# Attention followed by a mixture of experts: the handover reordered, places read sooner, a quarter of GpSimd's descriptor space, two buffers of results, and rows of small blocks in portions

## The chip, the cores and the metric

The kernel runs on one core of a Trainium2 chip. The metric is the device time of one execution in microseconds (us), as the median of several. Before the change three runs took 877.47, 880.67 and 881.1 us. One more execution was profiled; the rows quoted here come from it. Engines go by these names: PE is TensorE (PEld its weight loads), DVE is VectorE, ACT is ScalarE, POOL is GpSimd, SP is the engine that only issues transfers. A `q` behind an engine's name means its instruction queue.

## The reference

Inputs are q, k and v of 8 batches, 12 heads, 448 tokens and 64 columns in float32, a cap of 30, a router of 768 x 8 and, for 8 experts, w1 of 768 x 1024 and w2 of 1024 x 768.

```
scores = scale * q @ k^T;  scores = cap * tanh(scores / cap)
attn = exp(scores - max) / (sum + 1e-9);  y = attn @ v
x = y as 3584 tokens x 768
logits = x @ w_gate;  e = argmax(logits);  gate = softmax(logits)[e]
out[token] = gate * (relu(x @ w1[e]) @ w2[e])
```

Every token goes to one expert, so how many tokens an expert gets is known only after the router has seen them.

## The kernel before, in words

**Attention.** There are 8 batches of 6 pairs of heads, 48 pairs, each one step `n` of a loop. In a step TensorE makes the scores of a pair (L253, L260), ScalarE takes tanh and exp (L264, L273; one exponential of 128x1792 a pair for the first two thirds, one of 128x896 for the rest), VectorE and GpSimd add the probabilities for the row sums (`adds`, L282 on VectorE, L290 on GpSimd), TensorE multiplies with v into PSUM (`pv`, L309, L320), and VectorE copies the result out of PSUM (L336) and transposes it (`turn`, L347). The engines run an order that is written out by hand: each engine takes its instructions in the order in which the program issues them. Other work is hung into this loop with `at(step, when, function, ...)`; `do(step, when)` issues it. Within a step the order of the places is 0, scores, products with v of the pair before, 5, `adds` of the first half, second scores, loads, 3, second products with v, 6, `adds` of the second half, 1, 2.

**Routing.** Once a batch's six pairs are done (its step `n` is then the first of the next batch) it is normalised, routed and stored: `rec_v`, `rec_p`, `rec_c` (reciprocal sums), `log_v`, `log_p` (logits), `route_v` (argmax, L466 to L480), `place_p` (TensorE counts tokens before each one, L517 and L519), `place_v` (VectorE: each token's place in its expert's list, L529 to L538, which also moves `base`, the counts so far), `scale` (L505), `store` (rows to the DRAM array `xd`, on SP's queue) and `place_d` (GpSimd scatters the tokens' numbers into the DRAM lists `ids`, four indirect transfers a batch, L544). `log_p`, `place_p` and the router's products L372 share one PSUM bank, `ps_l`.

**Blocks.** The experts' work is cut into blocks of 448 tokens (large) or 256 (small) of one expert each. Two early blocks, -1 and -2, are chosen before attention is over (`first_block`, spread over steps by `decide`): -1 from the first 4 batches, so that its rows and weights are there when attention ends; -2 from the first 6. All later blocks come from a table made at the end; here their order is 0 to 4 (large), then two small ones. For a block, `load_ids` reads its part of the lists (an indirect transfer into `idt`, waiting for the scatters issued before it), `make_idx` turns it into row numbers (VectorE, L874), `load_x` gathers its rows into `xg` (14 indirect transfers for a large block, 8 for a small one, L802), `trans_x`, `high_x` and `low_x` transpose them and split them into a high and a low part (L910, L913, L917), and `load_w0` (SP, early blocks) or `load_w` (GpSimd, four indirect transfers) fetches weights, which `high` and `low` split (L843, L848). `up` is the first product with its relu (18 matmuls, L940; L945, L946), `down` the second (L970, L978), each in eight chunks. `evac` brings the result from PSUM into the tile `ys` (L1003, L1013), and `put` scatters it to the output (L812).

**The handover.** After step 47 the program goes on with block -1 by hand: `up(-1, 0)` while the last batch is still being routed, with the splits of the weights, the gathers of block -2 (`load_x(-2, ...)`) and the last batches' `place_d` between them.

**The expert loop.** While block j computes, GpSimd gathers the next block's rows and stores the results of the one before. In large blocks `moves` spreads both over the chunks: `XS` and `PS` say how many groups of rows go out at which chunk, and `step`, a one-column copy on GpSimd that reads a chunk's activation, holds GpSimd back until that chunk is there (L952).

Of the kernel before, what the change touches and what calls it, by code (L numbers as in the profile page):

```python
# [4 lines left out]
F32 = mybir.dt.float32  # L5
# [121 lines left out]
def attention_moe(tc, qT, kT, vL, capd, wgL, w1a, w1b, w2a, w2b, cst, cmk, out):  # L127
# [768 lines left out]
    def load_x(j, gs=None):  # L896
        xi = idt[j][0]
        rows = 4 * S * (B_FIRST[-1 - j] if j < 0 else B)
        for g in gs or range(groups(j)):
            gather(xg[:, g, :], xd[0:rows, :], xi[:, g : g + 1], rows - 1)  # L900
# [87 lines left out]
    def evac(j, cs=range(2)):  # L988
        y = m["y"]
        if cs[0] == 0:  # L990

            ys[j] = (
                ys0
                if j == -1
                else xg.rearrange("p q x -> p (q x)")
                if j == ORDER[-2]
                else m["yo"].tile([128, QB * XW], F32, name="ys")
            )
        o = ys[j]
        if large(j):  # L1000
            ov = o.rearrange("p (q k i) -> p q k i", k=KC, i=32)
            for k in range(KC):
                V.transpose(out=ov[:, :, k, :], in_=y[k][:, 0:LARGE].rearrange("p (q j) -> p q j", j=32))  # L1003
        else:
            ov = o[:, 0 : 2 * DM].rearrange("p (c a k i) -> p c k a i", c=2, a=4, i=32)
            for c in cs:
                for half in range(2):
                    src = y[2 * c + half][:, 0:384].rearrange("p (k a i) -> p k a i", a=4, i=32)
                    dst = ov[:, c, 3 * half : 3 * half + 3]
                    if half == 0:  # L1010
                        A.copy(out=dst, in_=src)
                    else:
                        V.tensor_copy(out=dst, in_=src)  # L1013
# [19 lines left out]
    def at(step, when, f, *a):  # L1033
        tasks.setdefault((step, when), []).append((f, a))
# [5 lines left out]
    for b in range(B):  # L1040

        n = b * NP + NP
        for g in range(1, NP, 2):
            i = b * NP + g
            at(i + 2, 5, sums, i)
        at(n, 5, logits, b, range(4))
        at(n + 1, 3 if b == B - 1 else 5, logits, b, range(4, NP))
        if b == B - 1:
            break
        at(n + 1, 6, rec_v, b)  # L1050
        at(n + 2, 3, rec_p, b)
        at(n + 2, 6, rec_c, b)
        at(n + 3, 0, log_v, b)
        at(n + 3, 6, log_p, b)
        at(n + 3, 1, route_v, b)
        at(n + 4, 5, route_s, b)
        at(n + 4, 3, place_p, b)
        at(n + 4, 6, route_g, b)
        at(n + 4, 1, scale, b, 0, V)
        at(n + 5, 0, scale, b, 1, V)  # L1060
        at(n + 5, 2, store, b, range(0, 2))
        at(n + 5, 1, place_v, b)
        at(n + 6, 2, store, b, range(2, 4))
        if b < B - 2:
            for q in range(4):
                at(n + (7 if b < 4 else 11 if b == 4 else 7), 1, place_d, b, q)
    at(1, 1, constants)
    at(n_first, 1, lambda: [None for _ in first_block(0)])
    at(n_first, 2, first_row, 0)
    for i in range(2 * FC):  # L1070
        at(n_first + 1 + i, 2, load_w0, -1, i)
    at(n_first + 2, 2, load_ids, -1)
    at(n_first + 3, 1, make_idx, -1)

    g = 0
    for i, w in enumerate((5, 5, 4)):
# [1 line left out]
        g += w  # L1078


    for n, k, last in ((8, 0, 1), (7, 1, 1), (6, 2, 1), (6, 3, 1), (4, 4, 2), (4, 5, 2)):
        at(n_pairs - n, 2, trans_x, -1, k)
        at(n_pairs - n + 1, 5, high_x, -1, k)
        at(n_pairs - n + last, 1 if last == 1 else 3, low_x, -1, k, V)
    at(n_pairs - 2, 2, split_w1, 0, G)

    second = first_block(1)

# [1 line left out]
        for _ in range(k):  # L1090
            next(second, 0)

    for n, k in ((6, 6), (4, 8), (1, 4)):
        at(n_pairs - n, 6, decide, k)
    at(n_pairs, 0, split_w1, 1, G)
    at(n_pairs, 6, decide, 100)
    for q in range(4):
        at(n_pairs, 1, place_d, B - 2, q)
    at(n_pairs, 1, load_ids, -2)

    for i in "hl":
        m["x" + i] = xp.tile([128, KC, LARGE], F32R, name="x" + i)
# [62 lines left out]
    do(n_pairs + 1, 3)  # L1165
    assert not tasks
    split(1, 2)
    make_idx(-2)
    load_x(-2, range(3))
    up(-1, 1)  # L1170
    rec_p(b)
    rec_c(b)
    log_v(b)
    split(1, 3)
    up(-1, 2)
    step(-1, 2)
    load_x(-2, range(3, 5))
    split(1, 4)
    log_p(b)
    route_v(b)  # L1180
    route_s(b)
    up(-1, 3)
    step(-1, 3)
    load_x(-2, range(5, 8))
    place_p(b)
    split(1, 5)
    place_v(b)
    up(-1, 4)
    step(-1, 4)
    load_x(-2, range(8, 10))  # L1190
    split(2, 0)
    turn(n_pairs - 2)
    turn(n_pairs - 1)
# [2 lines left out]
    w2s[3] = chunk(hw2, "w23")  # L1196
    up(-1, 5)
    step(-1, 5)
    load_x(-2, range(10, 12))
    split(2, 1)  # L1200
    route_g(b)
    scale(b, 0, V)
# [13 lines left out]
    wb = m["yo"] = pools("wb", **tw)  # L1216
    w2s[4] = chunk(wb, "w24")
    w25h = wb.tile([128, DM], F32R, name="w25h")
    ys0 = wb.tile([128, QB * XW], F32, name="ys")
    w26l = wb.tile([128, DM], F32R, name="w26l")  # L1220
    w2s[5] = [w25h, wb.tile([128, DM], F32R, name="w25l")]
    w2s[6] = [wb.tile([128, DM], F32R, name="w26h"), w26l]
# [4 lines left out]
    fill(4)  # L1227
    up(-1, 6)
    step(-1, 6)
    load_x(-2, range(12, 14))  # L1230
    for q in range(4):
        place_d(b, q)
    split(2, 5)
# [59 lines left out]

    XS, PS = (3, 3, 3, 3, 2, 0, 0), (0, 1, 1, 2, 2, 4, 4)

    def moves(j, n0, n1, f):
        if f > 0:
            step(j, f + 1)
        for load, n, what in ((True, n1, XS), (False, n0, PS)):
            g = sum(what[:f])  # L1300
            gs = range(g, min(g + what[f], groups(n) if load else QB))
            if load and gs:
                load_x(n, gs)
            elif gs:
                put(n, gs=gs)

    for i, j in enumerate(blocks):
        if i == 0:
            continue
        n0 = blocks[i - 1]  # L1310
        n1 = blocks[i + 1] if i + 1 < len(blocks) else None
        n2 = blocks[i + 2] if i + 2 < len(blocks) else None
        up(j, 0)
        if i == 1:
            splits(*late[0][:1])
        up(j, 1)
        splits_after(i, 0)
        if n1 is not None:
            make_idx(n1)
            load_w(n1, 1 if i > 1 else 0)  # L1320
            if not large(j):
                load_x(n1)
        if n2 is not None and not large(j):
            load_ids(n2)
        for f in range(FC):
            if large(j) and f < len(XS):
                moves(j, n0, n1, f)
            if 0 < f:
                splits_after(i, f)
                if f == 2 and i == 1:  # L1330
                    load_w(n1, 1)
            if n1 is not None:
                splits_in(i, f)

            down(j, f, range(2) if n1 is not None or f < 3 else range(1))
            if f + 2 < FC:
                if f + 2 == FC - 1 and n1 is not None:
                    for k in range(XT):
                        trans_x(n1, k)
                up(j, f + 2)  # L1340
            if f + 2 == FC and n1 is not None:
                split_xs(n1)
            if f == 4:
                if n2 is not None:
                    if large(j):
                        load_ids(n2)
                if not large(j):
                    put(n0)
            if f == (6 if i == 1 else 4) and n2 is not None:
                load_w(n2, 0)  # L1350
        if n1 is not None:
            evac(j)
# [93 lines left out]
```

## Time and profile before

| | |
|---|---|
| runs | 877.47, 880.67, 881.1 us |
| profiled execution | 879.77 us, span 877.8 us |
| TensorE | 830.4 us busy, 4492 matmuls |
| VectorE | 556.9 us busy |
| ScalarE | 483.4 us busy |
| GpSimd | 460.5 us busy |
| mean granted TensorE clock | 0.984 |
| moved | 117.96 MB |

The span runs from the first to the last instruction; the rest of an execution's time lies around it. Attention takes the first 370 us or so, the experts the rest. The chain of work that ended last is TensorE for 53% of the span. In rows of the timeline the first two numbers are the start and the duration, and brackets hold the idle time of the engine just before the instruction and what ended it. In rows of waits stand the waiting engine and line, what it waited for, the total, the number of times and the longest.

### The profile page before, as it was taken

How to read it: one execution, taken by the hardware profiler on the slowest of the kernel's cores; microseconds unless marked ns; L12 is line 12 of the kernel's file. 1: busy time of each engine (PE TensorE's matmuls, PEld its weight loads, DVE VectorE, ACT ScalarE, POOL GpSimd, SP SyncE). 2: the span in 40 equal slices, each digit the busy share in tenths (PEclk: the TensorE clock that was granted, in tenths of full speed). 3: DMA queues.
4: the chain of work that ended last, by engine and by line, in shares of the span. 5: the costliest groups of instructions: out<-in, count | busy, mean ns of one | idle time of the engine just before them, and what ended most of it. 6: DMA issues, size and time to landing. Idle time of an engine off the chain costs nothing.

```text
span 877.8 us, 12128 instructions
## 1 busy us (share of the span) xinstructions
PE 830.4 (95%) x4492; PEld 555.2 (63%) x4492; DVE 556.9 (63%) x912; ACT 483.4 (55%) x573; POOL 460.5 (52%) x380
## 2 busy tenths in 40 slices
PE   8999999999969999689999999999999999999993
PEld 3233332323222322169999989899999999999993
DVE  3559797979966899958682844734635536437620
ACT  7999998989876989413342532423323324233420
POOL 1423353434347654534348767578577675665710
PEclk9999999999999999899999999999999999999997
DMA  6131545555556655336645272454431124544210
GB/s 211 69 127 66 186 80 172 98 154 101 187 100 200 223 162 136 80 93 163 134 167 206 77 300 61 176 193 165 169 100 55 33 63 175 186 180 166 81 43 34
DMA packets 46883, 117.96 MB, mean 134 GB/s; under 512 B 8241, under 2 KB 27091, under 8 KB 43744
## 3 DMA queue, kind: packets, MB, share of 16 engines
q1 hardware_dynamic: 30688, 57.01, 23.5%
q0 software_dynamic: 15840, 59.86, 19.3%
q8 instruction: 37, 0.61, 0.3%
q14 instruction: 30, 0.25, 0.1%
q10 hardware_dynamic: 288, 0.23, 0.1%
HBM read 101.40 MB, written 22.36 MB: 141 GB/s over the span
## 4 chain that ended last, share of the span: by engine, by line
PE 53%; DVE 8%; issue 4%; POOL 2%; DMA 2%; ACT 1%; POOLq 0%; DVEq 0%; ACTq 0%
PE ph L940 23%; PE y L970 17%; PE y L978 4%; DVE p L282 2%; PE po L320 2%; PE sp L253 2%; DVE ys L1003 1%; PE po L970 1%; PE z L970 1%; DMA idt<-ids,ti 1%; POOL out L812 1%; DMA ids<-tok,slots 1%; DVE xl L917 1%; PE ps_l L970 1%; PE ps_s L970 1%
## 5 line engine op out<-in xcount | busy, mean ns | idle before, releaser
L290 POOL TENSOR_TENSOR p<-p,pr 64x896 f32<-64x896 f32 x47 | 107.3, 2282 | 189.8 <-DVE p L282 114.7
L945 ACT ACTIVATE hb<-ph 128x448 fp32r<-128x448 f32 (+1 forms) x69 | 35.1, 508 | 285.9 <-PE ph L940 197.4
L946 DVE SCALAR_TENSOR_TENSOR hb<-ph,hb 128x448 fp32r<-128x448 f32 (+1 forms) x69 | 39.4, 574 | 191.2 <-ACT hb L945 191.2
L264 ACT ACTIVATE pt<-sp,qsc 128x896 f32<-128x896 f32 x144 | 139.2, 1001 | 33.6 <-PE sp L253 33.0
L802 POOL DMA_INDIRECT xg<-xd,xi x114 | 136.5, 1198 | 37.8 <-issue 31.7
L253 PE MATMUL sp<-qr,kr 64*128 64x448 f32 x576 | 134.9, 572 | 3.0 <-ACT pr L264 1.5
L273 ACT ACTIVATE pt<-pt,capt 128x1792 f32<-128x1792 f32 x94 | 132.9, 1413 | 2.3
L320 PE MATMUL po<-pt,vr 128*64 128x448 f32 x576 | 130.9, 562 | 0.0
L812 POOL DMA_INDIRECT out<-ys,xi x98 | 107.7, 1099 | 29.2 <-issue 27.4
L253 PEld LDWEIGHTS sp<-qr,kr 64*128 64x128 f32 x576 | 47.1, 185 | 85.3 <-issue 46.7
L282 DVE TENSOR_TENSOR p<-pt 128x896 f32<-128x896 f32 x48 | 71.3, 1485 | 31.1 <-ACT pt L273 25.5
L320 PEld LDWEIGHTS po<-pt,vr 128*64 128x64 f32 x576 | 33.2, 137 | 79.3 <-issue 78.8
L282 DVE TENSOR_TENSOR p<-p,pt 128x896 f32<-128x896 f32 x48 | 54.5, 1135 | 20.7 <-ACT pt L273 19.8
L544 POOL DMA_INDIRECT ids<-tok,slots x32 | 36.4, 1136 | 12.6 <-issue 5.8
L913 ACT CAST xh<-xt 128x448 fp32r<-128x448 f32 (+1 forms) x54 | 27.0, 531 | 20.8 <-DVE xt L910 20.7
L336 DVE COPY ot<-po 128x448 f32<-128x448 f32 x48 | 29.5, 615 | 10.4 <-PE po L320 10.2
L309 PE MATMUL po<-pr,vr 64*64 64x448 f32 x192 | 27.3, 570 | 7.1 <-DVE ot L336 7.1
L802 POOL DMA_INDIRECT w1r<-in_w1b,widx x7 | 10.0, 1435 | 44.8 <-DVE w17l L848 44.5
L910 DVE STREAM_TRANSPOSE xt<-xg 128x448 f32<-128x448 f32 (+1 forms) x54 | 30.2, 584 | 0.8
L917 DVE TENSOR_TENSOR xl<-xt,xh 128x448 fp32r<-128x448 f32 (+1 forms) x54 | 28.8, 559 | 0.0
L1003 DVE STREAM_TRANSPOSE ys<-y 128x448 f32<-128x448 f32 x36 | 19.8, 613 | 13.2 <-DMA out<-ys,xi 7.7
L952 POOL COPY pace<-hb 128x1 f32<-128x1 f32 x40 | 13.7, 342 | 27.0 <-ACT hb L945 26.9
(420 smaller groups left out, 1946.1 us busy)
## 6 DMA issues: line engine op xcount, KB each, us to landing
vr<-in_vL SPq DMA_DIRECT2D x24, 448.0 KB, 6.1
kr<-in_kT SPq DMA_DIRECT2D x23, 448.0 KB, 3.4
qr<-in_qT SPq DMA_DIRECT2D x23, 448.0 KB, 4.6
xd<-yt SPq DMA_DIRECT2D x20, 336.0 KB, 6.5
xd<-w2r SPq DMA_DIRECT2D x12, 336.0 KB, 6.8
w1r<-in_w1a SPq DMA_DIRECT2D x8, 384.0 KB, 5.3
w1r<-in_w1b SPq DMA_DIRECT2D x8, 384.0 KB, 5.7
w2r<-in_w2a SPq DMA_DIRECT2D x8, 384.0 KB, 5.6
```

The source lines that it names most:

```text
L253: PE.matmul(sp[:, j, 0:S], kr[r, i, c], qr[r, i, :], start=True, stop=True)
L264: A.activation(out=x, in_=sp[:, 0:2, 0:S], func=AF.Tanh, scale=qsc)
L273: A.activation(out=pt[:, lo:hi, :], in_=pt[:, lo:hi, :], func=AF.Exp, scale=capt)
L282: V.tensor_tensor(out=p4, in0=pt[:, 0:2] if half == 0 else p4, in1=pt[:, 2 * half + 2 : 2 * half + 4], op=ALU.add)
L290: e.tensor_tensor(out=p4[r], in0=p4[r], in1=rests[n // 2][r], op=ALU.add)
L320: PE.matmul(po[64 * j : 64 * j + 64, 0:S], vr[:, n % 2 * 6 + 3 * j + t, :], pt[:, 2 * t + j], start=n == t == 0, stop=t == 2 and n > 0,)
L802: G.indirect_dma_start(out=dst, out_offset=None, in_=src, in_offset=bass.IndirectOffsetOnAxis(ap=idx.bitcast(U32), axis=0), bounds_check=b ...
L812: i = G.indirect_dma_start(out=dst, out_offset=bass.IndirectOffsetOnAxis(ap=idx.bitcast(U32), axis=0), in_=src, in_offset=None, bounds_che ...
L917: e.tensor_tensor(out=m["xl"][:, k, 0:n], in0=xts.pop((j, k)), in1=m["xh"][:, k, 0:n], op=ALU.subtract)
L940: PE.matmul(ph, w[:, c], x[:, k, 0:n], start=i == 0, stop=i == 3 * KC - 1)
L946: V.scalar_tensor_tensor(out=hl, in0=ph, scalar=0.0, in1=hh, op0=ALU.max, op1=ALU.subtract)
L970: PE.matmul(y[k][:, 0:LARGE], w[:, c], h, start=f == 0 and i == 0, stop=f == FC - 1 and i == 2)
```

## The change

Five things change at once.

- *Places read sooner.* `place_p` and `place_v` of every batch but the last change their order against the adds of their step (one later by most of a step, one a little sooner). The scatters of batch 3 go out two steps sooner, those of the other early batches at place 2 of the same step, and the list of block -1 is read one step sooner. In `decide`, and in the transposes and splits of block -1's rows, the steps are shared out anew.
- *Handover reordered.* The first two weight splits of w1 have their low part made by VectorE and not by GpSimd. The scatters of batch 6 are no longer issued before the list of block -2 is read, but after the gathers of its rows. `make_idx(-2)` and the first gathers stand after `log_v` of the last batch, and all fourteen gathers are out one chunk sooner.
- *A quarter of GpSimd's descriptor space.* `dynamic_dma_scratch_size` is 4096 bytes a partition; without the argument it is 16384.
- *Two buffers of results.* The tile `ys` gets two buffers of 10,752 bytes a partition.
- *Rows of small blocks in portions.* `moves` is used in small blocks too, with `XN` and `PN`: the next block's rows by two, the results of the large block before by 4, 5 and 5; a small block's results go out at chunk 4.

```diff
-                else m["yo"].tile([128, QB * XW], F32, name="ys")
+                else m["yo"].tile([128, QB * XW], F32, name="ys", bufs=2)
...
-        at(n + 4, 3, place_p, b)
+        at(n + 5, 5, place_p, b)
...
-        at(n + 5, 1, place_v, b)
+        at(n + 5, 6, place_v, b)
         at(n + 6, 2, store, b, range(2, 4))
         if b < B - 2:
             for q in range(4):
-                at(n + (7 if b < 4 else 11 if b == 4 else 7), 1, place_d, b, q)
+
+                at(n + (5 if b == B_FIRST[0] - 1 else 11 if b == 4 else 7), 2, place_d, b, q)
...
-    at(n_first + 2, 2, load_ids, -1)
-    at(n_first + 3, 1, make_idx, -1)
+    at(n_first + 1, 2, load_ids, -1)
+    at(n_first + 2, 1, make_idx, -1)
...
-    for n, k, last in ((8, 0, 1), (7, 1, 1), (6, 2, 1), (6, 3, 1), (4, 4, 2), (4, 5, 2)):
+    for n, k, late in ((8, 0, 0), (7, 1, 0), (6, 2, 0), (6, 3, 0), (6, 4, 1), (5, 5, 0)):
         at(n_pairs - n, 2, trans_x, -1, k)
-        at(n_pairs - n + 1, 5, high_x, -1, k)
-        at(n_pairs - n + last, 1 if last == 1 else 3, low_x, -1, k, V)
-    at(n_pairs - 2, 2, split_w1, 0, G)
+        at(n_pairs - n + 1 + late, 5, high_x, -1, k)
+        at(n_pairs - n + 1 + late, 1, low_x, -1, k, V)
+    at(n_pairs - 2, 2, high, 1, 0)
+    at(n_pairs - 1, 1, low, 1, 0)
...
-    for n, k in ((6, 6), (4, 8), (1, 4)):
+    for n, k in ((6, 3), (4, 10), (2, 6)):
         at(n_pairs - n, 6, decide, k)
-    at(n_pairs, 0, split_w1, 1, G)
+    at(n_pairs, 0, high, 1, 1)
     at(n_pairs, 6, decide, 100)
-    for q in range(4):
-        at(n_pairs, 1, place_d, B - 2, q)
     at(n_pairs, 1, load_ids, -2)
+    at(n_pairs, 1, low, 1, 1)
...
     split(1, 2)
-    make_idx(-2)
-    load_x(-2, range(3))
     up(-1, 1)
     rec_p(b)
     rec_c(b)
     log_v(b)
+    make_idx(-2)
+    load_x(-2, range(3))
...
-    load_x(-2, range(10, 12))
+    load_x(-2, range(12, 14))
+    for q in range(4):
+        place_d(b - 1, q)
...
-    load_x(-2, range(12, 14))
     for q in range(4):
         place_d(b, q)
...
+    XN, PN = (2, 2, 2, 2, 0, 0, 0), (0, 0, 0, 0, 4, 5, 5)
+
     def moves(j, n0, n1, f):
         if f > 0:
             step(j, f + 1)
-        for load, n, what in ((True, n1, XS), (False, n0, PS)):
+        xs, ps = (XS, PS) if large(j) else (XN, PN)
+        for load, n, what in ((True, n1, xs), (False, n0, ps)):
+            if n is None:
+                continue
+            if not load and not large(n):
+                if f == 4:
+                    put(n)
+                continue
...
-            if not large(j):
-                load_x(n1)
...
-            if large(j) and f < len(XS):
+            if f < len(XS):
                 moves(j, n0, n1, f)
...
-                if not large(j):
-                    put(n0)
...
-    nc = bacc.Bacc("TRN2", target_bir_lowering=False, num_devices=1)
+    nc = bacc.Bacc("TRN2", target_bir_lowering=False, num_devices=1, dynamic_dma_scratch_size=4096)
```

More of the change, by code (lines that the diff above doesn't have):

```diff
@@ L1176, in attention_moe @@
     step(-1, 2)
-    load_x(-2, range(3, 5))
+    load_x(-2, range(3, 6))
     split(1, 4)
@@ L1183, in attention_moe @@
     step(-1, 3)
-    load_x(-2, range(5, 8))
+    load_x(-2, range(6, 9))
     place_p(b)
@@ L1189, in attention_moe @@
     step(-1, 4)
-    load_x(-2, range(8, 10))
+    load_x(-2, range(9, 12))
     split(2, 0)
@@ L1218, in attention_moe @@
     w25h = wb.tile([128, DM], F32R, name="w25h")
-    ys0 = wb.tile([128, QB * XW], F32, name="ys")
+    ys0 = wb.tile([128, QB * XW], F32, name="ys", bufs=2)
     w26l = wb.tile([128, DM], F32R, name="w26l")
```

## The prediction

> **What bounds the kernel now.** I read the busy time by stretch first, then GpSimd, VectorE and TensorE in order of time where TensorE is not full, then the list of waits. Columns of the first view: stretch, length, busy time (and instructions) of TensorE, weight load, VectorE, ScalarE and GpSimd, then granted clock, DMA share, GB/s.
>
> ```profile
> 0.00:240.00 240.00, 232.70 (x1338) 73.19 (x1340) 183.47 (x283) 215.97 (x206) 87.88 (x49) 1.00 0.46 133
> 240.00:300.00 60.00, 52.43 (x289) 15.74 (x287) 41.58 (x68) 45.24 (x43) 38.52 (x26) 0.94 0.57 157
> 300.00:360.00 60.00, 53.43 (x316) 16.48 (x312) 56.03 (x101) 54.10 (x56) 27.20 (x17) 1.00 0.49 144
> 360.00:400.00 40.00, 30.96 (x162) 21.48 (x155) 26.32 (x53) 8.92 (x14) 21.00 (x17) 0.87 0.44 106
> 400.00:860.00 460.00, 456.75 (x2380) 424.52 (x2380) 249.00 (x409) 158.70 (x256) 283.94 (x271) 1.00 0.40 137
> ```
>
> Attention up to 240 us keeps TensorE 97% and ScalarE 90% busy; the experts from 400 to 860 us keep TensorE 99% busy. There, an edit can win only the 3.25 us that are missing. The loose time lies between: 7.6 us idle in 240 to 300, 6.6 in 300 to 360, 9.0 in 360 to 400, and two of these stretches also run at a granted clock below 1. The parts below are ordered by the place they touch.
>
> **The change part by part.** Sums go against the profiled execution: span 877.8 us, 879.77 with what lies around it, 0.9 below the 880.67 median of the three runs shown.
>
> *A. Places read sooner, first early block.* Time, duration, engine, line; in brackets idle time before it and its releaser.
>
> ```profile
> 219.53 1.07 DVE L282 TENSOR_TENSOR p<-p,pt 128x896 f32<-128x896 f32 x1
> 237.64 2.09 POOL L290 TENSOR_TENSOR p<-p,pr 64x896 f32<-64x896 f32 x1 [7.53 <-DVE p L282]
> 241.38 1.07 DVE L282 TENSOR_TENSOR p<-p,pt 128x896 f32<-128x896 f32 x1
> 243.60 0.97 POOL L544 DMA_INDIRECT ids<-tok,slots  x1 [0.30 <-DVE lt L427]
> 244.88 0.92 POOL L544 DMA_INDIRECT ids<-tok,slots  x1 [0.30 <-issue]
> 249.98 1.79 ACT L273 ACTIVATE pt<-pt,capt 128x1792 f32<-128x1792 f32 x1
> 253.50 1.05 POOL L802 DMA_INDIRECT idt<-ids,ti  x1 [4.93 <-DMA ids<-tok,slots]
> 257.43 1.79 ACT L273 ACTIVATE pt<-pt,capt 128x1792 f32<-128x1792 f32 x1
> 259.30 0.23 DVE L874 TENSOR_SCALAR xi<-idt,kc 128x14 int32<-128x14 int32 x1 [7.64 <-DMA idt<-ids,ti]
> 263.11 1.76 PE L309 MATMUL po<-pr,vr 64*64 64x448 f32 x4 [7.12 <-DVE ot L336]
> 269.43 1.01 ACT L264 ACTIVATE pt<-sp,qsc 128x896 f32<-128x896 f32 x1 [10.21 <-PE sp L253]
> 273.34 1.79 ACT L273 ACTIVATE pt<-pt,capt 128x1792 f32<-128x1792 f32 x1
> DMA to landing us min/median/max: 6.8/8.9/13.8
> ```
>
> The last `place_d` of batch 3 is issued at 244.88 and lands by 253.5; only then may GpSimd read the list (`load_ids`), which lands at 259.3. VectorE stands 7.64 us in `make_idx`, with the PSUM copies of attention queued behind it, so TensorE stands 7.12 and then ScalarE 10.21. From one long exponential (L273, one a pair of heads) to the next this pair takes 273.34 - 257.43 = 15.91 us, the pair before it 257.43 - 249.98 = 7.45, so the stall is worth 8.5, and 10.2 if ScalarE's wait counts whole.
>
> Afterwards `place_v` of batch 3 stands before the add at 219.53, which moves that add to about 220.5, and its four `place_d` go out behind GpSimd's add of 2.1 us, from about 224 on, 1.28 apart (244.88 - 243.60), the last one at 228. They land (median 8.9) at 237, at worst at 242. `load_ids` follows GpSimd's add that ends at 239.7, and takes 5.8 (253.5 to 259.3) as here: 245.5, or 248 behind late scatters. VectorE asks for it after its add that ends at 242.45. A wait of 3 us remains, 5.5 at worst; ScalarE runs a pair ahead of VectorE here (its exponential of 249.98 is used by the add after 259.30), which hides part of such a wait. Putting the stall's whole worth at 10.2 and what still shows at 1.7, I take 8.5; the bounds are 3.0 (8.5 - 5.5) and 10.2. The five GpSimd issues move ahead of two of its adds, which start some 5 us later; TensorE reads those adds a pair (7 us) later.
>
> After A's stall the 240 to 300 row shows a clock of 0.94. The Trainium skill, "TensorE: Matmul & The Clock Gate" (Part 1: The HAM clock gate), puts the drop to half rate after an idle window of about 3.4 us; by it the remaining wait of 3 costs no clock. The trace agrees with the long stalls (7.12 us idle, then 0.06 x 60 = 3.6 us of clock lost); if the remainder still set it off, A would be 3.6 less, by the row, 4.9.
>
> *F. `place_p` and `place_v` swapped around, all batches.*
>
> ```profile
> PE ps_l L372 <- DVE base L531: 8.9, 5, 5.8
> PE ps_l L517 <- DVE ob L480: 4.4, 3, 2.4
> ```
>
> Waits in total, times, longest. The router matmul L372 reuses the bank that `place_v` reads; `place_v` now precedes an add instead of following it. The place matmul L517 moves most of a pair later and stops waiting for its one-hots. Without the two longest (C, B) that is 3.1 + 2.0 = 5.1 of TensorE time. ScalarE at 90% is close behind, so I take 2.0 (0 to 5.1).
>
> *B. Steps 42 to 47.* The 2.4 wait above (it falls at 351) disappears; two row transposes, their splits and four small decisions move ahead by one or two pairs. VectorE is 56.03 of 60 us busy in 300 to 360, so it gives little back: 1.5 (0 to 2.4).
>
> *C. End of attention: the first two weight splits leave GpSimd.*
>
> ```profile
> 362.19 3.12 POOL L848 TENSOR_TENSOR w10l<-w1r,w10h 128x768 fp32r<-128x768 f32 x1
> 363.57 4.46 DVE L282 TENSOR_TENSOR p<-pt 128x896 f32<-128x896 f32 x1
> 369.61 1.72 PE L372 MATMUL ps_l<-ot,wg 128*32 128x448 f32 x8 [5.81 <-DVE base L531]
> 372.87 0.47 PE L940 MATMUL ph<-xh,w10h 128*128 128x448 f32 x1
> 380.07 0.95 DVE L848 TENSOR_TENSOR w12l<-w1r,w12h 128x768 fp32r<-128x768 f32 x1
> ```
>
> VectorE's add takes 4.46 against 1.07 for its like (241.38) while GpSimd makes w10l and then w11l; behind it `place_v` is late, and TensorE stands 5.81. Both splits now cost VectorE 0.95 each (w12l), behind `place_v`; TensorE needs them for its first two expert products, the second one 3.7 us after the first. The add returns 3.4, `place_v` loses the decisions ahead of it: L372 starts near 365.7, 3.9 sooner, and L372 with the last products runs at full clock (3.26 from 369.61 to 372.87; about 2 undisturbed). 5.2 in all; at least 2 if the add stays slow for another reason, at most 5.81 + 1.3 = 7.1.
>
> *D. Second early block: places of batch 6 no longer before its list; `make_idx` behind `log_v`.*
>
> ```profile
> 382.40 1.05 POOL L802 DMA_INDIRECT idt<-ids,ti  x1 [6.68 <-DMA ids<-tok,slots]
> 385.78 0.23 DVE L874 TENSOR_SCALAR xi<-idt,kc 128x14 int32<-128x14 int32 x1 [4.76 <-DMA idt<-ids,ti]
> 389.51 0.49 PE L446 MATMUL ps_l<-lr,cs 128*128 128x112 f32 x2 [3.23 <-DVE lr L441]
> 395.34 7.55 PE ph L940 x36
> 417.52 3.72 PE ph L940 x18
> ```
>
> The list waits 6.68 for four scatters it does not need, VectorE 4.76 for the list, TensorE 3.23 for `log_v`. From 372.87 four first products end at 395.34: 22.5 us. At 3.7 each (417.52) they need 14.9, and the products between them (12 of the width of L372, of which 8 took 1.72 at a reduced clock, and some small ones) at most 2.6: 17.5; I leave 0.4 for the split that now follows `make_idx`: 4.6 (1.7 to 5.0). The list has 10 us until VectorE asks, against 3.4 (382.40 to 385.78). The four scatters stand later on GpSimd, after all 14 row gathers; nothing of this block reads them, and the next list still waits for those of batch 7 behind them. SP's loads for this block wait, as before, for the splits that free their slots. The row gathers queue behind `make_idx`, now some 6 us sooner than at 385.78.
>
> *E. Two result buffers.*
>
> ```profile
> PE y L970 <- DVE hb L946: 1.9, 2, 1.1
> PE y L978 <- DVE hb L946: 1.2, 1, 1.2
> 502.76 3.29 DVE L1003 STREAM_TRANSPOSE ys<-y 128x448 f32<-128x448 f32 x6
> 562.59 3.31 DVE L1003 STREAM_TRANSPOSE ys<-y 128x448 f32<-128x448 f32 x6 [3.70 <-DMA out<-ys,xi]
> 621.28 3.30 DVE L1003 STREAM_TRANSPOSE ys<-y 128x448 f32<-128x448 f32 x6 [2.56 <-issue]
> 796.29 3.30 DVE L1003 STREAM_TRANSPOSE ys<-y 128x448 f32<-128x448 f32 x6 [2.92 <-PE ph L940]
> ```
>
> Block results wait for the stores of the block before them; behind this wait stands the copy that the next products need, and TensorE loses 0.8 + 1.1 + 1.2 = 3.1. The 0.8 (502.76) had no wait ahead of it, only splits, and stays: 2.3 (0 to 3.1).
>
> *Portions for small blocks.* The gathers and stores of the two small blocks are spaced by `step`; they stay under the small blocks' products, and the end is set by the last products and their stores, which keep their order: 0. Without that cover the last stores come later by a portion of five, 5 x 1.28 = 6.4 us.
>
> *A quarter of the descriptor space.*
>
> ```profile
> DMA to landing us min/median/max: 2.1/3.5/10.3
> w2r<-in_w2b,widx POOLq DMA_INDIRECT x7, 9.8
> w1r<-in_w1b,widx POOLq DMA_INDIRECT x7, 7.6
> POOL w1r L802 <- DVE w17l L848: 44.5, 6, 8.6
> ```
>
> GpSimd issues 1.28 us apart (A) and gathers land within 10.3, so 8 are under way at most. No row shows an issue that waits for space: the old space held 8 or more, a quarter of it 2 or more. Taken at 0, as nothing queues on the whole; the price when it doesn't is the second rival. The Trainium skill, "DMA: Bandwidth & Descriptors" (The descriptor swizzle), counts 9 read and 9 write descriptors per engine for a 128-partition transfer, of 16 bytes; 4,096 bytes would then hold, as an estimate, 14 to 28 transfers, and the cost stays 0.
>
> Sum: 8.5 + 2.0 + 1.5 + 5.2 + 4.6 + 2.3 = 24.1; 879.77 - 24.1 = 855.7. All lower bounds: 6.7, giving 873.1; all upper ones: 32.9, giving 846.9.
>
> **The rivals.** *Half the stalls move on.* The scatters of A land at the slow end (13.8) and VectorE, full in 300 to 360, stays the bound up to 370: A 3.0, B 0, C 2, the others whole: 13.9, 865.9. For it speaks VectorE's 56 of 60; against it that its longest instruction there loses its cause.
>
> *Descriptor space runs short: slower.* If a pair of weight gathers plus rows fill the quarter, GpSimd stands until they land. A block of 58.7 us (562.59 to 621.28) holds 33 issues (14 gathers, 14 stores, one list, four weights) of 1.28 = 42, so 16.5 are free, 7.4 of them (44.5 / 6) in one wait before w1b. Both weight pairs awaited cost 2 x (7.6 + 9.8 - 2.6) = 29.6, 13.1 over, in six blocks 79: 935. It decides once such waits add up to over 16.5 a block. Against it: 8 under way, and gathers whose rows are single long pieces.
>
> *ScalarE sets attention's pace, and the handover only shifts idle time to the experts:* A and F give 3, C and D are lost again to late weights (loads and splits of the second block don't start sooner): within 0.5%, about 877. Against it: TensorE is full from 400 on without waiting for weights.
>
> **How the numbers follow.** Forecast 855.7 with its own range 848 to 862: 0.64. Half the stalls: 0.2. Descriptor space: 0.07. Nothing gained: 0.06. The remaining 0.03 is a faster end below 848. The range 848 to 867 takes in the first two. Half a per cent, about what a measurement tells from no change, is 4.4 us: faster 0.87, same 0.06, slower 0.07.
>
> **What would show it.** A: no wait over 3 us before `xi` near 242, clock 1.00 in 240 to 300. C: the add before `place_v` near 1.1 us, no GpSimd row of L848. D: no TensorE wait for `lr`. E: no wait of L1003 for stores. Space: waits before GpSimd issues beyond 0.3. It is wrong if the span between the last exponential and the first full expert product doesn't shrink by some 10 us.

## The result and the profile after

The changed kernel takes **852.12 us** (median of four runs, 850.72 to 854.53) beside 879.07 for the kernel before on the same chip (875.05 to 881.1): ratio 0.9705, 95% interval 0.9671 to 0.9739. The profiled execution took 851.22 us with a span of 849.2, 28.7 less than before (877.84 and 849.16 unrounded); the forecast was 24.1 less. Two later series with both kernels gave 0.9615 (0.9583 to 0.9647) and 0.9687 (0.9657 to 0.9716).

Busy time by stretch of the kernel after; the columns are those of the prediction's first view.

```profile
0.00:240.00 240.00, 236.01 (x1348) 73.93 (x1348) 184.40 (x287) 218.09 (x208) 93.83 (x54) 1.00 0.47 131
240.00:300.00 60.00, 58.51 (x340) 18.18 (x342) 52.53 (x82) 53.74 (x52) 37.00 (x23) 1.00 0.59 197
300.00:360.00 60.00, 54.00 (x294) 17.80 (x287) 57.32 (x103) 46.47 (x48) 26.31 (x16) 0.94 0.51 131
360.00:400.00 40.00, 39.61 (x212) 34.31 (x211) 29.18 (x67) 11.58 (x18) 24.09 (x23) 1.00 0.62 165
400.00:830.00 430.00, 428.76 (x2238) 399.98 (x2237) 232.50 (x373) 152.38 (x245) 273.83 (x272) 1.00 0.41 136
```

The hole in 240 to 300 is closed (58.51 where 52.43 stood), that in 360 to 400 too (39.61 and 30.96). One is left: 300 to 360 still has 6.0 us without TensorE and now loses clock as well.

To see which part brought what, one mark on TensorE's timeline was taken at each stage's border. Kernel before, then kernel after: first half scores of the first pair, scores of pairs 29, 37 and 47, the first expert product of block -1, its first second product, the last matmul of the program. (Block -1's first product of the kernel before, at 372.87, stands in the prediction.)

```profile
8.91 1.08 PE L260 MATMUL sp<-qr,kr 64*64 64x448 f32 x8 [0.95 <-ACT pt L264]
...
209.12 1.77 PE L253 MATMUL sp<-qr,kr 64*128 64x448 f32 x8
...
277.75 1.77 PE L253 MATMUL sp<-qr,kr 64*128 64x448 f32 x8
...
354.89 1.77 PE L253 MATMUL sp<-qr,kr 64*128 64x448 f32 x8
...
402.73 0.57 PE L970 MATMUL z<-yt,w20h 128*128 128x448 f32 x2
...
863.81 0.34 PE L978 MATMUL y<-w27h,hb 128*128 128x384 f32 x1
```

```profile
10.31 1.08 PE L260 MATMUL sp<-qr,kr 64*64 64x448 f32 x8 [0.95 <-ACT pt L264]
...
208.30 1.77 PE L253 MATMUL sp<-qr,kr 64*128 64x448 f32 x8
...
267.06 1.77 PE L253 MATMUL sp<-qr,kr 64*128 64x448 f32 x8
...
342.87 1.77 PE L253 MATMUL sp<-qr,kr 64*128 64x448 f32 x8
...
357.20 0.74 PE L940 MATMUL ph<-xh,w10h 128*128 128x448 f32 x1
...
383.59 0.56 PE L970 MATMUL z<-yt,w20h 128*128 128x448 f32 x2
...
840.90 0.34 PE L978 MATMUL y<-w27h,hb 128*128 128x384 f32 x1
```

The differences between neighbouring marks are the stages. A, for one, is (277.75 - 209.12) - (267.06 - 208.30) = 68.6 - 58.8. The last column does the same for the two kernels on another chip (second series, below).

| stage | part | forecast | measured | second pair |
|---|---|---|---|---|
| start to the first mark | | 0 | -1.4 | -1.4 |
| to pair 29 | F | 2.0 | 2.2 | 2.3 |
| pairs 29 to 37 | A | 8.5 | 9.9 | 7.5 |
| pairs 37 to 47 | B | 1.5 | 1.3 | 2.7 |
| pair 47 to the first expert product | C | 5.2 | 3.7 | 2.0 |
| to the first second product | D | 4.6 | 3.5 | 4.4 |
| to the last matmul | E | 2.3 | 3.8 | 7.5 |
| after the last matmul | none | 0 | 5.8 | 5.6 |
| sum | | 24.1 | 28.7 | 30.7 |

Taken together attention and the handover gave 20.6 where the forecast had 21.8. (The first row is left out of this: the first mark lies anywhere between 8.7 and 10.3 us in the profiles of the changed order.) The forecast was too low above all by what comes behind the last matmul, which no part of it named. There, these are GpSimd's last issues, of before (shown first) and after:

```profile
865.53 0.97 POOL L812 DMA_INDIRECT out<-ys,oi  x1 [4.30 <-DVE ys L1013]
```

```profile
843.21 0.97 POOL L812 DMA_INDIRECT out<-ys,oi  x1 [4.88 <-issue]
```

From that issue to the end of the span it was 877.8 - 865.5 = 12.3 us, now 849.2 - 843.2 = 6.0. The profile does not count what GpSimd does in that time as busy; the record of its single instructions has it (start and duration in us, the kernel before and the kernel after; the two names are those of the last two longer instructions there):

```
before  INC_SWDGE_SEM 869.68 1.57    DRAIN 871.29 5.71    end of span 877.84
after   INC_SWDGE_SEM 847.21 0.35    DRAIN 847.59 0.73    end of span 849.16
```

The time from the last issue to the first of the two is nearly the same, 4.1 and 4.0 us; the two themselves take 7.28 and 1.08.

### The profile page after: what moved, and what is told of

It reads as the page before. It is cut to its first block, busy times and chain, and to the rows that moved or that the text cites. A ratio compares the mean times of both kernels' runs of the same rounds, so it can differ in the third digit from the quotient of the medians.

```text
span 849.2 us, 12136 instructions
## 1 busy us (share of the span) xinstructions
PE 828.1 (98%) x4492; PEld 555.1 (65%) x4492; DVE 557.9 (66%) x914; ACT 484.0 (57%) x573; POOL 458.3 (54%) x390
## 4 chain that ended last, share of the span: by engine, by line
PE 78%; DVE 11%; ACT 6%; issue 3%; POOL 1%; DMA 1%; POOLq 0%; DVEq 0%; ACTq 0%
PE ph L940 26%; PE y L970 20%; PE sp L253 10%; PE po L320 9%; DVE p L282 3%; PE y L978 2%; ACT pt L264 2%; PE po L309 2%; ACT pt L273 2%; PE ps_s L358 2%; PE sp L260 2%; PE ps_l L372 1%; PE po L970 1%; PE z L970 1%; DVE xl L917 1%
## 5 line engine op out<-in xcount | busy, mean ns | idle before, releaser
L946 DVE SCALAR_TENSOR_TENSOR hb<-ph,hb 128x448 fp32r<-128x448 f32 (+1 forms) x69 | 39.8, 578 | 199.1 <-ACT hb L945 198.9
L253 PE MATMUL sp<-qr,kr 64*128 64x448 f32 x576 | 137.1, 580 | 3.2 <-ACT pr L264 1.6
L282 DVE TENSOR_TENSOR p<-pt 128x896 f32<-128x896 f32 x48 | 81.4, 1696 | 31.7 <-ACT pt L273 25.4
L282 DVE TENSOR_TENSOR p<-p,pt 128x896 f32<-128x896 f32 x48 | 53.0, 1103 | 15.6 <-ACT pt L273 14.7
L952 POOL COPY pace<-hb 128x1 f32<-128x1 f32 x52 | 17.3, 332 | 27.8 <-ACT hb L945 27.5
L917 DVE TENSOR_TENSOR xl<-xt,xh 128x448 fp32r<-128x448 f32 (+1 forms) x54 | 28.7, 560 | 0.0
L264 ACT ACTIVATE pr<-sp,qsc 128x896 f32<-128x896 f32 x24 | 23.9, 995 | 2.9 <-PE sp L260 2.9
```

What stands on the lines that cost most here:

```text
L253: PE.matmul(sp[:, j, 0:S], kr[r, i, c], qr[r, i, :], start=True, stop=True)
L264: A.activation(out=x, in_=sp[:, 0:2, 0:S], func=AF.Tanh, scale=qsc)
L282: V.tensor_tensor(out=p4, in0=pt[:, 0:2] if half == 0 else p4, in1=pt[:, 2 * half + 2 : 2 * half + 4], op=ALU.add)
L946: V.scalar_tensor_tensor(out=hl, in0=ph, scalar=0.0, in1=hh, op0=ALU.max, op1=ALU.subtract)
```

## The experiments

Three series, each on one chip with runs of the kernel before in it. Its median was 894.19 us in the first (chip A), 897.23 in the second (B) and 880.38 in the third (C). The changed kernel itself ran on B (862.36) and C (851.90), not on A; kernels of A are compared by stages with one another. Where nothing else is said, an edit is made to the changed kernel.

### The kernel before, again, and the changed kernel on two more chips

Edit: none.

> The kernel before, unchanged, with a profile of its own beside the other runs of this series. In the first series of experiments it took 894.19 us (median), 15 more than the 879.07 beside which the changed kernel was first timed, and the kernel before with only the smaller descriptor space had, in its profile there, ScalarE standing 8.3 us near 830 us in the last small block but one and TensorE 4.6. Theory chip: the extra time belongs to a chip, and this kernel is back at 877 to 882 on another one, or at 890 to 897 on the same one. Theory program: it belongs to the order of the small blocks' row transfers and the profile shows the stall again between 815 and 845 us wherever it is slow.

> The changed kernel, unchanged, so that the other runs of this series have a partner on their own chip. Theory chip: it moves with the kernel before, ratio again 0.967 to 0.974. Theory program: it takes 850.7 to 855 wherever the kernel before is, and its ratio falls to 0.955 where that one is slow.

> The changed kernel, unchanged, as the partner of the other three on their chip. If the extra time near 820 us belongs to the chip and the store bursts together, it takes 851 to 855 where TensorE shows no gap over 1 us after 780, and 859 to 866 where it shows one.

The kernel before took 896.94 us on B, the changed one 862.36 there (859.92 to 865.95) and 851.90 on C (851.19 to 853.76). So on B both are slower than at first, the old one by 18 and the new one by 10. In both, TensorE has gaps on B between 815 and 845 us, beside others, and none of those over 1 us in the first comparison or, for the changed kernel, on C. Both theories held in part: the extra time is of a chip or session, and how much of it a kernel gets depends on its small blocks, as the next run shows.

### Small blocks' rows all at once again

```diff
-        xs, ps = (XS, PS) if large(j) else (XN, PN)
...
-            if f < len(XS):
+            if large(j) and f < len(XS):
                 moves(j, n0, n1, f)
...
+                if not large(j):
+                    put(n0)
```

> The changed kernel, with only the small blocks' row gathers and stores issued all at once again, as before the change. The prediction's theory, portions are worth nothing: within 1 us of the changed kernel of this series, no TensorE gap over 1 us between 780 and 845. The rival, fourteen stores in one go starve the other engines: TensorE gaps that sum to 5 to 15 us near 800 to 820, and a time 5 to 15 above the changed kernel on a chip on which the kernel before is slow, 0 on another.

866.81 us (864.92 to 870.58) on B, 4.45 above the changed kernel; by stages, 4.25 of it lies between the first second product and the last matmul, and no other stage differs by over 0.6. Timeline of this run, GpSimd, ScalarE and TensorE:

```profile
801.11 1.03 POOL L812 DMA_INDIRECT out<-ys,xi  x1 [0.31 <-issue]
...
818.15 0.97 POOL L812 DMA_INDIRECT out<-ys,xi  x1 [0.31 <-issue]
...
821.65 0.38 ACT L945 ACTIVATE hb<-ph 128x256 fp32r<-128x256 f32 x1 [12.57 <-remote]
...
822.09 0.69 PE L978 MATMUL y<-w27h,hb 128*128 128x384 f32 x1 [8.06 <-ACT hb L945]
```

The same in the changed kernel on the same chip:

```profile
820.18 0.97 POOL L812 DMA_INDIRECT out<-ys,xi  x1 [0.30 <-issue]
...
823.12 0.69 PE L978 MATMUL y<-w20h,hb 128*128 128x384 f32 x1 [3.02 <-ACT hb L945]
```

While GpSimd issues fourteen stores in one go, ScalarE stands for 12.57 us, the product it waits for being long done ("remote" is a releaser that the profile doesn't know), and TensorE for 8.06 behind it. They go on some 2.5 and 3 us after the issue of the last store. With the portions the stall is 3.02 and comes later in the program, again at the last of the stores. So the portions are worth 4.4 us on this chip. Elsewhere no run takes them out alone; that the prediction's 0 holds where the stall doesn't occur is argued from the first profile of the kernel before, in which the same stores ran without one.

### Stores spread wider

```diff
-(0, 0, 0, 0, 4, 5, 5)
+(0, 0, 0, 0, 2, 3, 3)
...
+                if f < 3:
+                    put(blocks[-3], gs=range(8 + 2 * f, 10 + 2 * f))
```

> The changed kernel with the fourteen row stores of the last large block spread over both small blocks (2, 3, 3 in the first, 2, 2, 2 in the last) in place of 4, 5, 5 in the first. Theory, a long run of back-to-back row transfers of GpSimd holds up the other engines: where the partner shows a TensorE gap near 820, this one has none over 1 us after 780 and takes 3 to 7 less; where the partner shows none, both take the same within 1. Rival, it is the number of stores and not their density, or the place in time: the gap moves into the last block, same time within 1.5.

852.06 us (850.58 to 853.69) on C, the same as its partner there. But the partner had no TensorE gap after 780 us on that chip, so the run says only that spreading costs nothing; what makes the stall is left open by it.

### A quarter of the descriptor space alone

```diff
-    nc = bacc.Bacc("TRN2", target_bir_lowering=False, num_devices=1)
+    nc = bacc.Bacc("TRN2", target_bir_lowering=False, num_devices=1, dynamic_dma_scratch_size=4096)
```

(The kernel before with this one line.)

> The kernel before with the quarter of descriptor space alone. The trace of after ends 7.9 us behind TensorE's last product, that of before 13.7: GpSimd's last bookkeeping takes 0.35 and 0.73 us there against 1.57 and 5.71. Theory: these two depend on the size of the descriptor space, so this kernel gains 6.0 us (879.1 to 873), with the same chain of products, and its GpSimd rows at the end take about 0.4 and 0.7. Rival 1: the end was shorter because of the order of the last stores; then no change (879 within 2), rows at the end as before. Rival 2: a small space makes GpSimd wait for room before issues: waits over 0.3 us before its transfers, and not faster.

884.64 us (880.1 to 887.47) on A, ratio to the kernel before 0.9894 (0.9844 to 0.9945). After the last matmul its profile has 7.7 us, as the changed kernel has (7.9), where the kernel before has 13.7. In the single instructions, INC_SWDGE_SEM took 0.37 and DRAIN 0.81. So the space alone makes that end. The rest of the difference, 9.5 against 6.0, is within the spread on this chip (the interval reaches from 5 to 14 us), on which this kernel also shows the stall of the small blocks:

```profile
825.00:833.00 8.00, 3.78 (x18) 2.53 (x16) 3.26 (x6) 1.85 (x3) 6.17 (x7) 1.00 0.22 77
833.00:840.00 7.00, 2.73 (x9) 2.73 (x10) 2.46 (x4) 2.75 (x6) 1.40 (x2) 0.52 0.09 30
```

### A sixteenth of the descriptor space

```diff
-dynamic_dma_scratch_size=4096)
+dynamic_dma_scratch_size=1024)
```

> The changed kernel with a quarter of its descriptor space again: 1,024 bytes in place of 4,096. The prediction's theory, nothing queues on the whole: within 1.5 us of the partner, GpSimd's idle time before its gathers and stores stays 0.3 a piece, and at most the 1.1 us that are left of the bookkeeping at the end of the program can go. Rival, the space decides once it is short: waits of microseconds before GpSimd's issues, first in the small blocks where it issues every 1.28 us, weights late, and 10 to 80 us more.

851.97 us (848.13 to 852.8) on C against 851.90: the same. The waits of GpSimd from 700 us on, where it issues most densely, with 1,024 bytes:

```profile
POOL out L812 <- issue: 12.2, 37, 0.7
...
POOL xg L802 <- issue: 3.4, 13, 0.3
```

50 issues waited 15.6 us in all, 0.3 a piece, none over 0.7. The space is not short at a sixteenth either, so the second rival was far off; and DRAIN took 0.65, so what a smaller space can save was saved.

### Places of the first early block late again

```diff
-    at(n_first + 1, 2, load_ids, -1)
-    at(n_first + 2, 1, make_idx, -1)
+    at(n_first + 2, 2, load_ids, -1)
+    at(n_first + 3, 1, make_idx, -1)
```

(And batch 3's scatters two steps later, as before.)

> The changed kernel with the scatters of batch 3, the reading of the first early list and its use in their old steps; place_p and place_v stay as changed. Theory: VectorE's wait of over 7 us before xi and TensorE's gap of about 7 are back, clock below 1 near 260: 8.5 to 10.1 us slower, 860.6 to 862.2. Rival: the earlier place_v alone shortens the wait, as the scatters could land sooner: under 5 us slower, below 857.

861.99 us (860.5 to 863.34) on A. Beside the kernel of the next experiment, on the same chip and with the same code up to the experts, its pairs 29 to 37 take 69.9 and not 59.2 us, 10.7 more, and between the first mark and the experts no other stage differs by over 0.4. (The 59.2 is a low one: this stage takes 58.8 to 62.4 us in the changed order, so beside a higher one the difference would be 7.6.) The stall is back where it was:

```profile
262.48 1.76 PE L309 MATMUL po<-pr,vr 64*64 64x448 f32 x4 [8.01 <-DVE ot L336]
```

### One result buffer

```diff
-"ys", bufs=2)
+"ys")
```

> The changed kernel with one result buffer again. Theory: the waits of L1003 for stores come back (about 3.7, 3.2, 2.1, 2.0, 2.9 us), TensorE gets back two gaps of 1.1 to 1.2 us, so 2.3 to 2.8 us slower than 852.1: 854.4 to 854.9. Rival: the stores are spaced otherwise now and the waits stay hidden: 852 within 1.

855.8 us (852.49 to 858.86) on A. From the first second product to the end of the last matmul it takes 461.8 us, the two kernels of this chip that keep both buffers 460.1 and 460.0: the second buffer is worth 1.7 to 1.8 there. The waits of L1003 are back, 11.6 us in all, and two of TensorE's gaps, though at 0.61 and 0.68 and not at the 1.1 and 1.2 expected. The line's own summary shows its waits; one buffer:

```profile
L1003 DVEq EVENT_SEMAPHORE  x24: 49/50/3795, 481.6 to 773.6; - x24
...
its engine sat idle before it (us, times) until:
  DMA out<-ys,xi: 6.5, 3
  PE ph L940: 3.1, 1
  issue: 2.0, 1
```

With two, in the changed kernel, the 36 transposes stand alone and no idle time is listed before them:

```profile
L1003 DVE STREAM_TRANSPOSE ys<-y x36: 601/610/645, 483.7 to 774.4; 128x448 f32<-128x448 f32 x36
```

### First two splits on GpSimd again

```diff
-    at(n_pairs - 2, 2, high, 1, 0)
-    at(n_pairs - 1, 1, low, 1, 0)
+    at(n_pairs - 2, 2, split_w1, 0, G)
...
-    at(n_pairs, 0, high, 1, 1)
+    at(n_pairs, 0, split_w1, 1, G)
...
-    at(n_pairs, 1, low, 1, 1)
```

> The changed kernel with the low parts of the first two weight chunks made by GpSimd again. Theory: VectorE's add of pair 47 takes 4 us or more again, place_v is late, TensorE waits 4 to 6 us for it: 4 to 5.5 us slower, 856 to 857.6. Rival: in the changed kernel VectorE is full without a gap from 311 to 359 us, so 1.9 us less work for it pays for the contention: between 851 and 853.

860.17 us (858.79 to 862.33) on A. Against the run with one buffer the stage from pair 47 to the first expert product is 4.3 longer (17.0 and 12.8), the one before it 1.4; another 2.6 lies in pairs 29 to 37, which the edit doesn't reach and which vary from run to run (see the clock, further down). That is what put it above the 857.6 expected. Its GpSimd, VectorE and TensorE:

```profile
354.92 3.12 POOL L848 TENSOR_TENSOR w10l<-w1r,w10h 128x768 fp32r<-128x768 f32 x1
358.01 1.79 POOL L848 TENSOR_TENSOR w11l<-w1r,w11h 128x768 fp32r<-128x768 f32 x1
...
356.29 4.46 DVE L282 TENSOR_TENSOR p<-pt 128x896 f32<-128x896 f32 x1
...
361.72 1.72 PE L372 MATMUL ps_l<-ot,wg 128*32 128x448 f32 x8 [4.98 <-DVE pos L533]
```

The add is at 4.46 again, and it ends 1.0 after the second split of GpSimd does (358.01 + 1.79 = 359.80; 356.29 + 4.46 = 360.75). In the kernel before it ended 1.0 behind the second split too (367.07 and 368.03). So it looks not slowed but held until both splits are done, and then run at its normal length. In the changed kernel the add at this place takes 1.08. The Trainium skill, "SBUF — State Buffer" (Who interferes with whom), states that VectorE and GpSimd share a pair of ports under an exclusive lock, and that a VectorE instruction with two inputs in SBUF contends for it with a GpSimd instruction that reads SBUF. The trace agrees.

### The second early block's list late again

```diff
+    for q in range(4):
+        at(n_pairs, 1, place_d, B - 2, q)
     at(n_pairs, 1, load_ids, -2)
...
+    make_idx(-2)
+    load_x(-2, range(3))
     up(-1, 1)
...
     log_v(b)
-    make_idx(-2)
-    load_x(-2, range(3))
```

> The changed kernel with only part D undone: the four scatters of batch 6 stand ahead of the second early block's list again, and its index list is made before log_v. By the two traces of before and after, D gave 3.5 of the 4.6 predicted: then this run takes 3 to 5 more than the changed kernel, and TensorE waits 3 us or more for lr near 370. Rival: at full VectorE load the wait only goes elsewhere (the first products of the second block wait for the splits either way): within 1 us of the changed kernel, and the wait for lr under 1.5.

874.73 us (871.9 to 875.53) on B, **12.4** above the changed kernel, where 3 to 5 was expected. The stage of D takes 39.8 us and not 25.7, 14.1 more; the stage before it is 3.9 shorter. GpSimd, VectorE and TensorE:

```profile
360.46 0.91 POOL L544 DMA_INDIRECT ids<-tok,slots  x1 [0.30 <-issue]
...
375.45 1.04 POOL L802 DMA_INDIRECT idt<-ids,ti  x1 [14.07 <-DMA ids<-tok,slots]
...
377.98 0.23 DVE L874 TENSOR_SCALAR xi<-idt,kc 128x14 int32<-128x14 int32 x1 [6.22 <-DMA idt<-ids,ti]
...
381.71 0.74 PE L446 MATMUL ps_l<-lr,cs 128*128 128x112 f32 x2 [5.33 <-DVE lr L441]
```

The last scatter is issued at 360.46 and the list has to wait until 375.4 for it; in the first profile of the kernel before this wait was 6.68. ScalarE waits 14.7 in the same time for a store of rows. D costs more here since C is in, and the trace shows how. With the splits out of the way TensorE reaches the expert products some 19 us earlier than in the kernel before on this chip (356.0 and 374.7). The scatters go out earlier by nearly as much (360.46 and 376.55 for the last one), but they now start 0.8 us behind the last of batch 6's row stores, and the two are in flight together (DMA share 0.99 from 355 to 360 us and 0.93 from 360 to 365). That store lands after 12.8 us and the last scatter after 14.2. In the two profiles of the kernel before the scatters start 4.4 us behind the last store, and the two land after 6.1 to 6.3 and 6.8 to 7.4. That stores and scatters hold each other up is read from this one trace; no run moves the one away from the other alone. Without D about half of what A to C gained, 9.8 of 18.7 us, would have been given back at this place.

### Attention's copies on ScalarE for five pairs

```diff
-            V.tensor_copy(out=ot, in_=po[:, 0:S])
+            if 42 <= n < 47:
+                A.copy(out=ot, in_=po[:, 0:S])
+            else:
+                V.tensor_copy(out=ot, in_=po[:, 0:S])
```

> The changed kernel with five of attention's copies out of PSUM (pairs 42 to 46, 0.6 us each) on ScalarE. Theory, VectorE without a gap sets the pace from 300 to 360 and this is why B lost 0.6 where 1.5 was forecast: VectorE gets 3.0 us back, TensorE's gap of 1.9 before L446 and the half clock behind it go, 2 to 4 us less than the partner. Rival, ScalarE (46 to 48 busy of 60 there) is as close a bound: its exponentials come later by the copies, VectorE waits for them, and the time is within 1 us of the partner or up to 3 above.

**848.33 us** (847.15 to 851.24) on C, 3.6 below the changed kernel's 851.90 (851.19 to 853.76); ratio to the kernel before 0.9652 (0.962 to 0.9685). Stages B and C are 1.0 and 2.0 shorter, together 87.7 us where the changed order takes 89.6 to 91.2 otherwise. The two profiles differ by 5.0 in all; 2.1 of it lies in pairs 29 to 37, ahead of the edit. (The 0.6 lost in B that the expectation speaks of was read from ScalarE's marks, which run ahead of TensorE's by varying amounts; by TensorE's, above, B gained 1.3.) The stretch from 300 to 360 and TensorE's wait for `lr` in it (the inserted lines move the numbers by 3):

```profile
300.00:360.00 60.00, 56.18 (x313) 19.14 (x310) 54.27 (x98) 48.57 (x54) 27.02 (x16) 1.00 0.57 140
```

```profile
333.60 0.48 PE L449 MATMUL ps_l<-lr,cs 128*128 128x112 f32 x2 [0.59 <-DVE lr L444]
```

VectorE falls from 57.8 in its partner to 54.3, TensorE rises from 53.6 to 56.2, the wait falls from 2.4 to 0.6, and the clock stays at 1.00. VectorE was the bound there, ScalarE had room. This version is the fastest of all that ran.

## Why the prediction was right

The forecast was 855.7 in a range of 848 to 867, and 852.1 came. Step by step:

**A** (8.5 forecast, 9.9 and 7.5 measured, 10.7 when it alone is undone, with the spread named there): right, and by its own working. Timeline of the kernel after, GpSimd and VectorE:

```profile
227.09 0.91 POOL L544 DMA_INDIRECT ids<-tok,slots  x1 [0.30 <-DVE cnt L586]
...
238.06 1.60 POOL L802 DMA_INDIRECT idt<-ids,ti  x1 [0.27 <-POOL p L290]
...
242.34 0.46 DVE L874 TENSOR_SCALAR xi<-idt,kc 128x14 int32<-128x14 int32 x1 [1.83 <-DMA idt<-ids,ti]
```

The last scatter went out at 227.1 (228 foreseen), the list was read at 238.1 behind GpSimd's add (239.7) and had landed at 242.3 (245.5). So VectorE's remaining wait was 1.83 and not 3.

**F** (2.0; 2.2 and 2.3): right. Its two waits, 3.1 and 2.0 up to 345 us, fell to 0.2 and 0. No run undoes it alone.

**B and C** (1.5 and 5.2; 1.3 and 3.7, second pair 2.7 and 2.0) were sized too high together: 6.7 was forecast, 5.0 and 4.7 came. Which of the two fell short is not shown, since the mark between them is a poor border. In the seven profiles whose code is the same up to the experts, C's stage takes 12.8 to 16.3 us and B's 74.4 to 76.9, in part by how much of a stretch of half clock falls before or behind the mark; the two together are steady at 89.6 to 91.2 (94.5 to 95.7 in the three profiles of the old order). Undone alone, C cost 4.3 + 1.4 = 5.7, no less than its forecast. Its cause was right: the add is back to 1.08 and `base` no longer late. What its step missed is that `place_v` still stands behind VectorE's other work. TensorE's stall at this place fell from 5.81 to 2.52, by 3.3 and not by the 3.9 of the step:

```profile
352.43 1.08 DVE L282 TENSOR_TENSOR p<-pt 128x896 f32<-128x896 f32 x1
...
354.48 1.10 PE L372 MATMUL ps_l<-ot,wg 128*32 128x448 f32 x8 [2.52 <-DVE pos L533]
```

and it is followed by 3.4 us at half clock (6.8 before), where the step had counted on full clock. B's wait of 2.4 for one-hots is gone; a wait for `lr` ahead of it stays (1.4 before and 2.0 after, in the second pair 2.5 and 1.9). B's ground, that a full VectorE gives little back, is what the run with the copies on ScalarE showed from the other side.

**D** (4.6; 3.5 and 4.4): right; no wait for `lr` is left at this place. The run that undid it showed what the sum by parts could not: C and D aren't independent, D is worth 14 once C is in, by the place at which the scatters then fall.

**E** (2.3; 1.7 to 1.8 when undone on A, 3.8 with all else that differs in that stage): right, down to the one gap that was to stay, 0.8 before and 1.1 now, before `down` near 486. What the other 2.0 of the 3.8 are is open; the second pair's 7.5 holds the 4.25 of the portions.

**The descriptor space** is the step that failed: it was taken at 0 because nothing queues. That reason was right (a sixteenth is no shorter), but the space also has a price at the end of the program, 5.8 us less here. It could not be read from the views the prediction used, which count GpSimd as idle there; the 13.7 us behind the last matmul were in the profile of before, and the prediction did not ask what they were. **Portions** at 0 missed 4.4 on B, the one chip on which they were undone.

**The signs** that the prediction named for A, C, D and E came: the waits are gone or short, and the add is short. Its clock of 1.00 from 240 to 300 came in this pair and not in five later profiles (see the clock, below). Its last sign, a stretch from the last exponential to the first expert products shorter by some 10 us, did not come. From the start of that exponential to the first of these products it was 372.87 - 362.48 = 10.4 us and is 357.20 - 350.64 = 6.6; to the first second product it was 40.3 and is 33.0. That is 3.8 or 7.3 less, and C and D together gave 7.1 of their 9.8. What A and E gave above their forecasts covered this shortfall, which is luck; the end of the program then put the span 4.6 us below the forecast. For the descriptor space it named waits before GpSimd's issues beyond 0.3 us. These occur in both kernels, up to 1.2 after and 1.5 before between the gathers and stores of rows, and tell nothing about the space.

Of the rivals, half the stalls moving on (865.9) came true only in part of B and C; the third fell, since the experts kept TensorE at 428.76 of 430.

**The clock.** The prediction expected no loss of clock from a remaining wait under 3.4 us, by a page of the Trainium skill. The runs say otherwise. In the kernel after, waits of 1.98 and 2.52 were each followed by one stretch of 3.41 us at a granted clock of 0.5; on C a wait of 1.56 before L446 near 244 was too, while one of 2.48 at that place on B was not.

The traces show what decides. In each of them the stretches of half clock begin and end on one grid of 3.413 us. From 30 us to the last matmul, and outside half clock, the fourteen traces have 33 cells of this grid in which TensorE was busy for 45% or less, and half clock followed every one. Of the 3,278 other cells, all busy for 49% or more, two were followed by it (54%, the one with the wait of 1.56, and 56%). The wait of 1.98 lay in one cell and left it at 1.50 of 3.41 us (44%); the one of 2.48 was split over two, at 79 and 49%. So, as an estimate from these traces, a wait costs clock once it fills over half of a cell: from 1.7 us on where it falls into one, and later where it is split. The Trainium skill, "TensorE: Matmul & The Clock Gate" (Part 1: The HAM clock gate), also has the window run freely, which fits this; that a whole idle window is needed does not fit. It also goes with the spread of pairs 29 to 37 in the ten profiles of the changed order: the wait near 244 varies from 1.3 to 3.1, and the stage takes 60.9 to 62.4 us in the five in which half clock follows, 58.8 to 60.6 in the others.

## What to carry to other kernels

Look at what lies behind the last matmul and behind the last store of a profile and ask which instruction fills it, even where every engine counts as idle: a fifth of this gain was there. When several waits follow each other on one handover, cost the chain and not each wait by itself: when the first is removed, the work behind it moves to another time and can meet other transfers there. Where VectorE is full, count an instruction of GpSimd beside it as VectorE time too (the add of 4.46 in place of 1.08), and move work to the engine with room. A wait shorter than a stretch of the clock can still cost half of one.

## What was not expected of the hardware

- **The end of this program pays for descriptor space.** GpSimd's last two steps took 7.28 us with 16,384 bytes, 1.08 to 1.18 with 4,096 and 0.98 with 1,024.
- **A stall of ScalarE, VectorE and TensorE during dense stores of GpSimd,** 3 to 12 us, on chips A and B, none on C and in the first comparison. In the traces of A and B some 25 to 29% of the semaphore events aren't recorded (they have 6,493 to 6,915, the others 9,162 to 9,182). So it may be the chip, or the recording on it; no run here separates the two, and nothing here shows what a run without a recording would take.
- **The kernel before varied by 18 us from series to series** (879.07, 880.38, 894.19, 897.23), the changed one by 10. Times count only beside others of their series, and the ratio itself moved, from 0.9705 to 0.9615 on B.
